# Half of the first layer's columns as seven products of quarters, in the third and later tiles of an attention and feed-forward kernel

## The chip, the cores and the metric

The kernel runs on one core of one Trainium2 chip. The metric is the device time of one execution in microseconds (us). The engines of the core have names in the profile: PE is TensorE, which multiplies matrices (PEld is its loading of weights), DVE is VectorE, ACT is ScalarE, POOL is GpSimd and SP is SyncE; here POOL and SP mostly issue transfers (DMAs). Each engine works through its own queue in order and waits at semaphores for the others. TensorE writes its results to PSUM, a small memory of eight banks; VectorE and ScalarE read them from there and write to SBUF, the working memory.

## The reference

```python
def _attn_ref(q, k, v, g_norm):                  # 8 batches, 8 heads, 576 rows, 64 columns
    kv = np.einsum('bhsd,bhse->bhde', k, v)
    out = np.einsum('bhsd,bhde->bhse', q, kv)
    rms = np.sqrt(np.mean(out * out, axis=-1, keepdims=True) + 1e-06)
    return out / rms * g_norm

def _moe_ref(x, w_in, w_out):                    # x: 4608 x 512, w_in: 512 x 2048, w_out: 2048 x 512
    h = x @ w_in
    g = h * (1.0 / (1.0 + np.exp(-1.702 * h)))
    return g @ w_out
```

The attention is linear: a 64 x 64 matrix `kv` for each head, multiplied by `q`, and each row of 64 scaled by its root mean square. The heads of a row are then laid side by side to a row `x` of 512, and two layers follow: `h = x @ w_in` with 2048 hidden columns, a gate (an approximate GELU), and `g @ w_out`.

## The kernel before

**Tiles.** The rows of `x` are worked on in tiles of 512: tile t (0 to 7) holds the first 512 rows of batch t, and tile 8 (the last) the 64 rows that are left of each of the eight batches, kept in `x_rem`. The text counts tiles from 0. Everything that TensorE multiplies is in f16, sums are f32.

**A tile.** The first layer (`Hidden`, L437) makes the hidden values transposed, with hidden columns on the partitions. A hidden column group ("column" in what follows, 128 of the 2048, so 16 columns) takes four matmuls of 512 moving columns at L446, one for each quarter `ko` of the 512 inputs, added up in one PSUM bank. ScalarE then applies the gate from PSUM into `gT` at L455. The columns run in the order 0, 8, 1, 9, and so on (L590).

The second layer (`Seven`, L463) is already a Strassen scheme for all tiles but the first. The 512 x 2048 by 2048 x 512 product is cut into quarters (256 rows, 1024 hidden values, 256 output columns) and done as seven products instead of eight. A product needs sums and differences of quarters: those of `w_out` are made once in `tw` (`weight_sum`, L457), those of `gT` for each tile in `gS` by VectorE (`sums`, L474). Each product is 16 matmuls of 256 moving columns at L551. The products run in the order 1, 5, 6, 2, 7, 3, 4 and share three PSUM banks: x collects products 1, 6, 7 and 4, y holds product 2, z products 5 and 3. After products 1, 5 and 6 ScalarE copies a bank to SBUF (`keep`, L521) as s1, s5 and s2; after products 2, 7 and 3 VectorE adds the kept part to the bank and writes the output tile `osb` (`place`, L529); after product 4 ScalarE copies the bank (L532). So TensorE must wait before it adds to a bank that is still being read.

**Attention between.** While tile t is worked on, the attention of batch t + 1 is made, in pieces that are hung into the order of the two layers by hand: `units1` after the i-th column of the first layer, `units2` after the n-th matmul of the second (112 in all). In the first layer these are the transposing DMA of q (`transpose_q`, L248), the repacking of k (`pack_k`, L218, two copies of VectorE into `kpad`), four blocks of `kv` (L226, nine small matmuls each; after the last one VectorE casts the result in four pieces, L246), and the loads of k, v and q for batch t + 2 on POOL's queue (L107 and L123). In the second layer these are four `rows` (L288, q times kv, then a square on ScalarE), their sums (L305), the roots (L315), `turn` (L320, scaling by VectorE and a transposing DMA to the next tile's x), and the left-over rows (`out`, `ss`, `apply`), which end in a write to `x_rem` at L360. Tile 7 has nothing left to prepare, and tile 8 neither.

**Scaling by g_norm.** In tiles 0 and 1 `g_norm` is multiplied into x. During the second layer of tile 1 it is multiplied into `w_in` instead, one quarter `ko` at a time (`scale_w_in`, L196): one quarter by ScalarE after matmul 48, three by VectorE after 80, 92 and 100. From tile 2 on x is left unscaled.

**Queues.** The order on every engine is the order of the program text (`manual_schedule`); semaphores come from the tiles' readers and writers. PSUM's eight banks are shared out as three for `ps_a` ("att"), three for `ps_h` ("hT") and two for `ps_o` ("o"). The output of a tile goes out on SP's queue, which also issues the transposing DMAs.

```python
        cols = range(FO) if deep else [f for i in range(HF) for f in (i, HF + i)]
        ready = {} if deep else {8: (0, 4), 13: (4, 6), 15: (6, 8, (0,))}
```

These two lines give the order of the columns and the column after which VectorE forms which part of `gS`.

Of the kernel before, what the change touches and what calls it, by code (L numbers as in the profile page):

```python
# [7 lines left out]
F16 = mybir.dt.float16  # L8
F32 = mybir.dt.float32
# [3 lines left out]
P = 128  # L13
# [3 lines left out]
def kernel(  # L17
# [61 lines left out]
    x_rem = const.tile([P, KO, B * R], F16)  # L79
    HF, HN = FO // 2, DM // 2  # L80
    tw = const.tile([P, 4, HF, HN], F16)


    raw = {"k": kraw, "q": qraw, "v": vbuf}
# [50 lines left out]
    first = {}  # L135
    for n in "kqv":
        if n != "q":
            rows = stage.tile([P, H, J * D], F32, name="qf", tag="qf")
# [298 lines left out]
    class Hidden:  # L437
# [16 lines left out]
        def gate(self, fo):  # L454
            nc.scalar.activation(self.gT[:, fo, :], self.h[fo], AFT.Gelu_apprx_sigmoid)  # L455

    def weight_sum(n):  # L457
        b11, b12 = w_out_sb[:, 0:HF, 0:HN], w_out_sb[:, 0:HF, HN:DM]
        b21, b22 = w_out_sb[:, HF:FO, 0:HN], w_out_sb[:, HF:FO, HN:DM]
        a, b = ((b12, b11), (b22, tw[:, 0]), (b22, b12), (b21, tw[:, 1]))[n]  # L460
        nc.vector.tensor_sub(tw[:, n], a, b)

    class Seven:  # L463
# [5 lines left out]
        def __init__(self, t, gT):  # L469
            self.t, self.gT = t, gT  # L470
            self.s = spool.tile([P, 4, HF, 2 * P], F16, name="gS", tag="gS")
            self.bank, self.kept = {}, {}

        def sums(self, i0, i1, which=(0, 1, 2, 3)):  # L474
            lo, hi = slice(i0, i1), slice(HF + i0, HF + i1)
# [39 lines left out]

        def keep(self, name, mo, as_):
            ps, m = self.ready(name, mo)
            if as_ not in self.kept:
                self.kept[as_] = attn.tile([P, 2, HN], F32, name=as_, tag=as_, bufs=1)
            if ps is not None:  # L520
                nc.scalar.copy(self.kept[as_][:, m], ps)  # L521

# [18 lines left out]

        def run(self, units2):
            n = 0
            for p in self.LAST if self.t == B else self.ORDER:
                name = {1: "x", 6: "x", 7: "x", 4: "x", 2: "y", 5: "z", 3: "z"}[p]
                split = self.t == B and name == "x"
                for mo in range(2):
                    o = self.banks(name, mo)
                    for i in range(HF):
                        a, w = self.operands(p, mo, i)  # L550
                        nc.tensor.matmul(  # L551
                            o,
                            a,
                            w,
                            start=(p in (1, 2, 5) and i == 0 and (mo == 0 or split)),
                            stop=(i == HF - 1),
                            skip_group_check=True,
                        )
                        if i == HF - 1:
                            step, *args = {  # L560
                                1: (self.keep, "s1"),
                                5: (self.keep, "s5"),
                                6: (self.keep, "s2"),
                                2: (self.place, "s1", 0, 0),
                                7: (self.place, "s5", 1, 1),
                                3: (self.place, "s2", 0, 1),
                                4: (self.place, None, 1, 0),
                            }[p]
                            step(name, mo, *args)
                        for u in units2.get(n, ()):  # L570
                            u()
                        n += 1

    def store_rest(mo, n0, n1):
        osb = osbs[B]
        for g in range(2):
# [6 lines left out]
            queue = (nc.sync, nc.scalar)[g]  # L583
            queue.dma_start(out=rows, in_=osb[g * R : (g + 1) * R, mo, n0:n1])

    def dense(t, units1, units2, group, deep, hid=None):
        hid = hid or Hidden(t)
        gT = hid.gT
# [3 lines left out]
        if group and t:  # L592
            order = [(ko, fo) for part in ((0, 3, 1, 2), range(4, group)) for ko in (0, 1) for fo in part]
            order += [(ko, fo) for ko in range(2, KO) for fo in range(group)]
            for ko, i in order:
                pool = (ps_h, "hT") if i < 3 else (ps_a, "att") if i == 3 else (ps_o, "o")
                hid.mm(ko, cols[i], *pool)
            for i in range(group):
                hid.gate(cols[i])
        for i, fo in enumerate(cols):  # L600
# [27 lines left out]
        if deep:  # L628
            steps = [(mo, 4 * i + k) for i in range(3) for mo in range(4) for k in range(4)]
            steps += [(mo, f + k) for f in (12, 14) for mo in range(2) for k in range(2)]  # L630
            steps += [(mo, 12 + k) for mo in (2, 3) for k in range(4)]
            for n, (mo, fo) in enumerate(steps):
                project(mo, fo)
                for u in units2.get(n, ()):
                    u()
        else:
            later = {6: [lambda: seven.sums(6, 8, (1,))], 30: [lambda: seven.sums(6, 8, (2, 3))]}
            for n, us in units2.items():
                later.setdefault(n, []).extend(us)
            seven.run(later)  # L640
# [102 lines left out]
    load_w_out(12, 14)  # L743
    load_w_out(14, FO)

    osbs = {}
    HALVED = (2, 3, 4, 5, 6)
    live = {0: a0}

    def start(b):  # L750
        live[b] = Second(b) if b == 1 else Attention(b)

    for t in range(NT):
# [3 lines left out]
        def at1(i, f, *args):  # L757
            u1.setdefault(i, []).append(lambda: f(*args))

        def at2(i, f, *args):  # L760
            u2.setdefault(i, []).append(lambda: f(*args))  # L761
# [28 lines left out]
        elif b < B:  # L790
            if t == 1:
# [60 lines left out]
```

## Time and profile before

| what | us |
|---|---|
| median of 3 runs (lowest, highest) | 277.36 (276.86, 277.59) |
| the profiled execution's own time | 278.32 |
| its span in the profile | 276.5 |
| TensorE busy | 268.6 (97%) |
| ScalarE busy | 165.9 (60%) |
| VectorE busy | 139.6 (50%) |
| first layer of tile 4, from its first matmul to the second layer's (134.80 to 149.66) | 14.86 |
| second layer of tile 4 (149.66 to 163.24) | 13.58 |
| first and second layer of tile 7, which has no attention work | 13.82 and 12.22 |

The profile is one execution. Its span goes from the first to the last instruction; what lies around it (1.82 us here) belongs to the measured time as well. A row of the groups gives line, engine, operation, output and inputs with their shapes and a count, then the busy time in all and the mean time of one in ns, then the idle time of the engine just before such an operation and what ended it. A row of the timeline or of the chain begins with start and length in us. The granted clock of TensorE was 0.993 of full speed over the span.

### The profile page before, as it was taken

Reading aid. Unit: us, or ns where it says so; the run is one execution under the profiler, and the core shown is the slowest. Engines: PE = TensorE matmul, PEld = TensorE weight load, DVE = VectorE, ACT = ScalarE, POOL = GpSimd, SP = SyncE. Lnnn points to the kernel's source line nnn. Section 1 sums busy time; section 2 is a strip of 40 time slices with the busy share of each in tenths; the row PEclk is TensorE's granted clock in tenths of the full one; section 3 lists DMA queues with packets and bytes.
Section 4 is the critical chain, followed back from the end, with each engine's and each line's share of the span. In section 5 each row is a group of like instructions: output and inputs, shape, how many; then the busy total and the mean of one; then the engine's idle time right before and its main releaser. Section 6 shows DMA issues by size and latency. Waiting matters only on the chain.

```text
span 276.5 us, 5263 instructions
## 1 busy us (share of the span) xinstructions
PE 268.6 (97%) x2160; PEld 173.8 (63%) x2160; DVE 139.6 (50%) x267; ACT 165.9 (60%) x281; POOL 49.9 (18%) x82
## 2 busy tenths in 40 slices
PE   8899999999999999999999999999999999999993
PEld 6434554458755786578646874687458845874682
DVE  1633364948653863377436742675167405222522
ACT  3568609858856765666566656675668466226610
POOL 8762353114010401040104010400000000000000
PEclk9989999999999999999999999999999999999999
DMA  8999999999659876968696869596600510011005
GB/s 173 183 199 204 205 204 199 257 148 156 94 106 216 119 112 153 190 96 114 131 205 108 110 145 208 85 120 180 137 0 2 151 76 2 0 79 76 1 2 152
DMA packets 56539, 35.27 MB, mean 128 GB/s; under 512 B 31810, under 2 KB 53826, under 8 KB 56386
## 3 DMA queue, kind: packets, MB, share of 16 engines
q0 software_dynamic: 25184, 17.91, 46.0%
q1 hardware_dynamic: 30848, 16.49, 24.3%
q10 hardware_dynamic: 482, 0.52, 0.6%
q8 instruction: 17, 0.28, 0.4%
q14 instruction: 8, 0.07, 0.1%
HBM read 36.70 MB, written 9.44 MB: 167 GB/s over the span
## 4 chain that ended last, share of the span: by engine, by line
PE 88%; ACT 3%; DMA 2%; DVE 2%; POOL 2%; issue 1%; DVEq 0%
PE hT L446 45%; PE o L551 32%; PE o L617 4%; PE kvp L230 3%; DMA w_in_sb<-in_moe_w_in_dram 2%; PE outR L294 2%; PE ss L342 1%; DVE x L322 1%; POOL qraw L90 1%; DVE w_in_sb L201 1%; ACT L761 0%; POOL kraw L90 0%; POOL vbuf L90 0%; PE outT L265 0%; DVE osb L529 0%
## 5 line engine op out<-in xcount | busy, mean ns | idle before, releaser
L446 PE MATMUL hT<-xT,w_in_sb 128*128 128x512 f16 x512 | 117.4, 381 | 1.0 <-DMA w_in_sb<-in_moe_w_in_dram 0.9
L455 ACT ACTIVATE gT<-hT 128x512 f16<-128x512 f32 x144 | 84.5, 601 | 40.9 <-PE hT L446 40.9
L446 PEld LDWEIGHTS <-w_in_sb 128*128 128x128 f16 x576 | 54.8, 98 | 62.6 <-issue 1.5
L485 DVE TENSOR_TENSOR gS<-gT 128x512 f16<-128x512 f16 (+1 forms) x48 | 24.4, 509 | 58.1 <-ACT gT L455 57.9
L551 PEld LDWEIGHTS <-gS 128*128 128x128 f16 x512 | 49.7, 98 | 5.8
L551 PE MATMUL o<-tw,gS 128*128 128x256 f16 x384 | 47.4, 273 | 0.0
L551 PEld LDWEIGHTS <-gT 128*128 128x128 f16 x384 | 37.1, 98 | 5.6
L551 PE MATMUL o<-w_out_sb,gT 128*128 128x256 f16 x256 | 33.5, 273 | 0.0
L529 DVE TENSOR_TENSOR osb<-o,s 128x512 f32<-128x512 f32 (+1 forms) x25 | 16.6, 665 | 15.0 <-issue 9.7
L109 POOL DMA_DIRECT2D kraw<-in_k_dram x16 | 9.9, 619 | 67.6 <-DVE kpad L221 61.6
L109 POOL DMA_DIRECT2D vbuf<-in_v_dram x16 | 9.7, 610 | 54.8 <-PE kvp L230 49.4
L521 ACT COPY s<-o 128x512 f32<-128x512 f32 (+1 forms) x26 | 14.3, 550 | 6.5 <-PE o L551 6.4
L344 ACT ACTIVATE ln<-ss,eps_t 128x512 f32<-128x512 f32 (+1 forms) x16 | 9.3, 581 | 14.7 <-PE ss L342 14.6
L322 DVE TENSOR_TENSOR x<-outR,sum 128x512 f16<-128x512 f32 x24 | 14.9, 684 | 6.1 <-ACT sum L318 6.1
L308 DVE TENSOR_REDUCE sum<-sq 128x8 f32<-128x512 f16 x24 | 16.2, 682 | 2.7 <-ACT sq L302 2.5
L246 DVE CAST kvd<-kvp 64x256 f16<-64x256 f32 x24 | 10.1, 422 | 13.9 <-PE kvp L230 13.6
L617 PE MATMUL o<-w_out_sb,gT 128*128 128x512 f16 x64 | 16.7, 379 | 0.0
L302 ACT ACTIVATE sq<-outR 128x512 f16<-128x512 f32 x24 | 14.4, 600 | 3.7 <-PE outR L294 3.7
L761 ACT ACT_TABLE_LOAD x12 | 15.4, 1283 | 0.2
L551 PE MATMUL o<-w_out_sb,gS 128*128 128x256 f16 x128 | 15.4, 272 | 0.0
L551 PE MATMUL o<-tw,gT 128*128 128x256 f16 x128 | 15.3, 273 | 0.0
L280 ACT ACTIVATE sq<-outT 128x512 f16<-128x512 f32 (+1 forms) x16 | 7.8, 493 | 12.3 <-PE outT L260 12.1
(76 smaller groups left out, 217.0 us busy)
## 6 DMA issues: line engine op xcount, KB each, us to landing
out_dram<-osb SPq DMA_DIRECT2D x10, 512.0 KB, 3.0
kraw<-in_k_dram POOLq DMA_DIRECT2D x12, 288.0 KB, 7.0
vbuf<-in_v_dram POOLq DMA_DIRECT2D x12, 288.0 KB, 4.8
qraw<-in_q_dram POOLq DMA_DIRECT2D x3, 512.0 KB, 8.3
qbuf<-in_q_dram POOLq DMA_DIRECT2D x3, 512.0 KB, 8.0
out_dram<-osb SPq DMA_DIRECT2D x6, 192.0 KB, 5.9
w_in_sb<-in_moe_w_in_dram POOLq DMA_DIRECT2D x4, 256.0 KB, 7.8
w_out_sb<-in_moe_w_out_dram POOLq DMA_DIRECT2D x2, 512.0 KB, 14.4
```

The lines of the kernel that those rows point to most:

```text
L109: nc.gpsimd.dma_start(out=raw[n][l * PH : (l + 1) * PH, c0:c1, 0 : NH * D], in_=srcs[n][b].rearrange("(c l) (p j) d -> l p c (j d)", l=2, ...
L302: nc.scalar.activation(sq, t, AFT.Square)
L308: nc.vector.tensor_reduce(out=self.sum4[:, j, :], in_=self.o[j][1].rearrange("p (x d) -> p x d", d=D), op=ALU.add, axis=mybir.AxisListType.X,)
L322: nc.vector.tensor_mul(self.x16[:, j0 : j0 + 2, c0 : c0 + DM // 2].rearrange("p l (h d) -> p h l d", d=D), self.o[j][0].rearrange("p (h l ...
L446: nc.tensor.matmul(self.h[fo], w_in_sb[:, ko, fo * P : (fo + 1) * P], self.x[:, ko], start=(ko == 0), stop=(ko == KO - 1),)
L455: nc.scalar.activation(self.gT[:, fo, :], self.h[fo], AFT.Gelu_apprx_sigmoid)
L485: op(s[:, n, lo], a, b)
L521: nc.scalar.copy(self.kept[as_][:, m], ps)
L529: nc.vector.tensor_add(o, ps, self.kept[with_][:, m])
L551: nc.tensor.matmul(o, a, w, start=(p in (1, 2, 5) and i == 0 and (mo == 0 or split)), stop=(i == HF - 1), skip_group_check=True,)
L617: nc.tensor.matmul(os[mo], gT[:, fo, mo * P : (mo + 1) * P], w_out_sb[:, fo, :], start=(fo == 0), stop=(fo == FO - 1),)
L761: u2.setdefault(i, []).append(lambda: f(*args))
```

## The change

From tile 2 on, eight of the sixteen columns of the first layer are no longer made one by one. Columns 2, 3, 10, 11 form one group and 6, 7, 14, 15 another (`PARTS`). In a group the product of a 512 x 512 piece of `w_in` with the tile's x is cut into quarters (256 inputs, 256 hidden values, 256 rows) and done as seven products of four matmuls with 256 moving columns each, in place of sixteen matmuls with 512 (`SevenIn`). A half column of the other eight (two matmuls of 512) stands between any two products (`hid_seven`).

The products need sums of quarters of `w_in` (`ws`, formed once by VectorE in the second layer of tile 1, `w_in_sum`) and differences of quarters of x (`xS`, formed by VectorE for each tile near the end of the second layer before, `Sums`). After products 1 and 6 ScalarE copies a bank to SBUF, after product 5 VectorE does; after products 2, 7 and 3 VectorE adds the kept part to the bank in SBUF and ScalarE applies the gate from there; after product 4 ScalarE applies it from the bank.

Around it some pieces move. `scale_w_in` on VectorE goes from matmuls 80, 92, 100 to 58, 65, 72. In tiles from 2 on the units of the first layer are counted in the 30 new steps: `transpose_q` and `pack_k` after step 3 instead of column 2, the kv blocks after steps 8, 10, 12 and 14 instead of columns 9 to 12, the loads after step 15 instead of column 13. The parts of `gS` are formed after other steps. The kept sums of both layers lie in the rotating tile "qf" of two buffers, and the second layer asks for its bank z first.

```diff
@@ declarations
+    KH, TH = KO // 2, SM // 2
+    PARTS = (2, 6)
+    ws = const.tile([P, 4, KH, 2 * len(PARTS) * P], F16)
@@ new functions
+    def quarters(w, f, k):
+        hi = slice(HF * P + f.start, HF * P + f.stop)
+        lower = slice(KH + k.start, KH + k.stop)
+        return w[:, k, f], w[:, lower, f], w[:, k, hi], w[:, lower, hi]
+
+    def w_in_sum(n):
+        for g, i in enumerate(PARTS):
+            a11, a12, a21, a22 = quarters(
+                w_in_sb, slice(i * P, (i + 2) * P), slice(0, KH)
+            )
+            o = [ws[:, m, :, 2 * g * P : 2 * (g + 1) * P] for m in range(4)]
+            op, a, b = (
+                (nc.vector.tensor_add, a21, a22),
+                (nc.vector.tensor_sub, o[0], a11),
+                (nc.vector.tensor_sub, a11, a21),
+                (nc.vector.tensor_sub, a12, o[1]),
+            )[n]
+            op(o[n], a, b)
+
+    class Sums:
+        def __init__(self, t):
+            x = xT[t] if t < B else x_rem.rearrange("p c (j r) -> p c j r", j=J)
+            self.x = [[x[:, k : k + KH, n : n + 2, :] for n in (0, 2)] for k in (0, KH)]
+            self.t = spool.tile([P, 4, KH, TH], F16, name="xS", tag="xS")
+
+        def form(self):
+            (b11, b12), (b21, b22) = self.x
+            t = [self.t[:, n].rearrange("p c (j r) -> p c j r", r=P) for n in range(4)]
+            for n, (a, b) in enumerate(((b12, b11), (b22, t[0]), (b22, b12), (b21, t[1]))):
+                nc.vector.tensor_sub(t[n], a, b)
+
+    class SevenIn:
+        ORDER = (1, 5, 6, 2, 7, 3, 4)
...
+        def gate(self, r, n, src):
+            to = slice(self.i + r * HF, self.i + r * HF + 2)
+            nc.scalar.activation(
+                self.gT[:, to, n * TH : (n + 1) * TH], src, AFT.Gelu_apprx_sigmoid
+            )
+
+        def product(self, p):
+            name = {1: "x", 6: "x", 7: "x", 4: "x", 2: "y", 5: "z", 3: "z"}[p]
+            if name not in self.bank:
+                pool, tag = (ps_o, "o") if name == "x" else (ps_a, "att")
+                self.bank[name] = pool.tile([P, 2, TH], F32, name="h7", tag=tag)
+            o = self.bank[name]
+            for a in range(2):
+                for k in range(KH):
+                    w, x = self.operands(p, a, k)
+                    nc.tensor.matmul(o[:, a], w, x, ...)
+            s = self.kept
+            if p == 1:
+                nc.scalar.copy(s["s1"], o)
+            elif p == 5:
+                nc.vector.tensor_copy(s["s5"], o)
+            elif p == 6:
+                nc.scalar.copy(s["s2"], o)
+            elif p == 4:
+                self.gate(1, 0, o)
+            else:
+                which, r, n = {2: ("s1", 0, 0), 7: ("s5", 1, 1), 3: ("s2", 0, 1)}[p]
+                nc.vector.tensor_add(s[which], o, s[which])
+                self.gate(r, n, s[which])
@@ the second layer: kept sums and banks
-            self.bank, self.kept = {}, {}
+            self.bank, self.kept = {}, None
...
-            if as_ not in self.kept:
-                self.kept[as_] = attn.tile([P, 2, HN], F32, name=as_, tag=as_, bufs=1)
+            if self.kept is None:
+                k = stage.tile([P, 6, HN], F32, name="qf", tag="qf")
+                self.kept = {s: k[:, 2 * i : 2 * i + 2] for i, s in enumerate(("s1", "s5", "s2"))}
...
             n = 0
+            self.banks("z", 0)
@@ the first layer of tile 2 and later
+    def hid_seven(t, hid, seven, units1):
+        pairs = [i for i in range(HF) if all(i not in (g, g + 1) for g in PARTS)]
+        halves = [(f, k) for i in pairs for f in (i, HF + i) for k in (0, KH)]
+        xs = xsums.pop(t)
+        steps = [halves[0], halves[1]]
+        for g in range(len(PARTS)):
+            part = SevenIn(hid, xs, g)
+            for n, p in enumerate(part.ORDER):
+                steps += [(part, p), halves[2 + g * len(part.ORDER) + n]]
+        for n, (f, k) in enumerate(steps):
+            if isinstance(f, SevenIn):
+                f.product(k)
+            else:
+                for ko in (k, k + 1):
+                    hid.mm(ko, f)
+                if k:
+                    hid.gate(f)
+            for u in units1.get(n, ()):
+                u()
+            which = {17: 0, 20: 1, 23: 2, 26: 3}.get(n)
+            if which is not None:
+                seven.sums(0, 4, (which,))
+        seven.sums(4, 8, (0,))
...
-            later = {6: [lambda: seven.sums(6, 8, (1,))], 30: [lambda: seven.sums(6, 8, (2, 3))]}
+            i = 4 if t >= SEVEN else 6
+            later = {6: [lambda: seven.sums(i, 8, (1,))], 30: [lambda: seven.sums(i, 8, (2, 3))]}
@@ where the pieces hang
-                at2(80, scale_w_in, 0, nc.vector)
-                at2(92, scale_w_in, 2, nc.vector)
-                at2(100, scale_w_in, 3, nc.vector)
-            f0 = 5 if t == 1 else 2
+                at2(58, scale_w_in, 0, nc.vector)
+                at2(65, scale_w_in, 2, nc.vector)
+                at2(72, scale_w_in, 3, nc.vector)
+                for n, at in ((2, 76), (0, 86), (1, 92), (3, 97)):
+                    at2(at, w_in_sum, n)
+            f0 = 5 if t == 1 else 3
+            late = 14 if t == 1 else 15
...
-                at1(14 if t == 1 else 13, load_kv, t + 2)
-                at1(14 if t == 1 else 13, load_q, t + 2)
+                at1(late, load_kv, t + 2)
+                at1(late, load_q, t + 2)
...
-                at1((10 if t == 1 else 9) + c, of(b, "kv", c))
+                at1(10 + c if t == 1 else 8 + 2 * c, of(b, "kv", c))
...
+            at2(100, form_sums, b)
+        elif t < B:
+            at2(100, form_sums, b)
```

More of the change, by code (lines that the diff above doesn't have):

```diff
@@ L137 @@
         if n != "q":
-            rows = stage.tile([P, H, J * D], F32, name="qf", tag="qf")
+            rows = stage.tile([P, 6, 2 * P], F32, name="qf", tag="qf")
             rows = rows.rearrange("p h x -> p (h x)")[0:PE_]
@@ new lines, with __init__, operands @@
+    class SevenIn:
+        ORDER = (1, 5, 6, 2, 7, 3, 4)
+        def __init__(self, hid, xs, g):
+            self.gT, self.xs, self.g, self.i = hid.gT, xs, g, PARTS[g]
+            self.bank = {}
+            k = stage.tile([P, 6, TH], F32, name="qf", tag="qf")
+            s12 = k[:, 0:4].rearrange("p (a n) c -> p a n c", n=2)
+            self.both = s12
+            self.kept = {"s1": s12[:, :, 0], "s2": s12[:, :, 1], "s5": k[:, 4:6]}
+        def operands(self, p, a, k):
+            f = slice((self.i + a) * P, (self.i + a + 1) * P)
+            g = slice((2 * self.g + a) * P, (2 * self.g + a + 1) * P)
+            a11, a12, a21, a22 = (w[:, 0] for w in quarters(w_in_sb, f, slice(k, k + 1)))
+            (b11, b12), (b21, b22) = [[x[:, k] for x in row] for row in self.xs.x]
+            t = [self.xs.t[:, n, k] for n in range(4)]
+            return {
+                1: (a11, b11),
+                2: (a12, b21),
+                3: (ws[:, 3, k, g], b22),
+                4: (a22, t[3]),
+                5: (ws[:, 0, k, g], t[0]),
+                6: (ws[:, 1, k, g], t[1]),
+                7: (ws[:, 2, k, g], t[2]),
+            }[p]
+        def gate(self, r, n, src):
[12 more added lines that the diff above has]
+                    w, x = self.operands(p, a, k)
+                    nc.tensor.matmul(
+                        o[:, a],
+                        w,
+                        x,
+                        start=(p in (1, 2, 5) and a == 0 and k == 0),
+                        stop=(k == KH - 1),
+                        skip_group_check=True,
+                    )
+            s = self.kept
[11 more added lines that the diff above has]
+                self.gate(r, n, s[which])
@@ L599, in dense @@
                 hid.gate(cols[i])
+        if t >= SEVEN:
+            hid_seven(t, hid, seven, units1)
+            cols = ()
         for i, fo in enumerate(cols):
@@ L744, with form_sums @@
     load_w_out(14, FO)
-    osbs = {}
+    osbs, xsums = {}, {}
+    SEVEN = 2
     HALVED = (2, 3, 4, 5, 6)
     live = {0: a0}
+    def form_sums(t):
+        xsums[t] = Sums(t)
+        xsums[t].form()
     def start(b):
```

## The prediction

> **What bounds the kernel now.** I read the busy shares first, then the chain that ended last, then the groups, then the timeline of one tile.
>
> ```profile
> span 276.5 us, 5263 instructions
> PE 268.6 (97%) x2160; PEld 173.8 (63%) x2160; DVE 139.6 (50%) x267; ACT 165.9 (60%) x281; POOL 49.9 (18%) x82
> PE 88%; ACT 3%; DMA 2%; DVE 2%; POOL 2%; issue 1%; DVEq 0%
> ```
>
> TensorE is busy for 97% of the span and carries 88% of the chain: time goes only if TensorE gets less to do, and comes back wherever TensorE waits.
>
> The chain in order of time (start, length, what) prices its work:
>
> ```profile
> 77.08 0.60 DVE osb L529
> 77.68 0.67 DVE w_in_sb L201
> 78.40 8.16 PE hT L446 x37
> ...
> 134.80 8.63 PE hT L446 x40
> 143.44 0.26 PE kvp L230 x9
> ...
> 220.12 13.81 PE hT L446 x64
> 233.94 12.23 PE o L551 x112
> ```
>
> A first layer without attention work is 64 matmuls in 13.81 us, 215.8 ns each (512 columns). A second layer, already made of 256-column matmuls, is 112 in 12.23, 109.2 ns each. The first rows show the one place where the vector engine already holds TensorE up, the end of the second tile. From the third tile on the steady tiles follow each other every 28.44 us (106.36, 134.80, 163.24).
>
> The groups give durations, the timeline the pace:
>
> ```profile
> L446 PEld LDWEIGHTS <-w_in_sb 128*128 128x128 f16 x576 | 54.8, 98 | 62.6 <-issue 1.5 <-DMA w_in_sb<-in_moe_w_in_dram 1.0 <-DVE w_in_sb L201 0.6
> L529 DVE TENSOR_TENSOR osb<-o,s 128x512 f32<-128x512 f32 x23 | 15.8, 686 | 14.4 <-issue 9.7 <-PE o L551 4.7
> L350 ACT ACTIVATE rs<-ln 128x512 f32<-128x512 f32 x8 | 5.0, 630 | 0.2
> ...
> 143.10 0.69 DVE L485 TENSOR_TENSOR gS<-gS,gT 128x1024 f16<-128x1024 f16 x1
> 143.71 0.68 DVE L485 TENSOR_TENSOR gS<-gT 128x1024 f16<-128x1024 f16 x1
> 147.11 1.74 DVE L246 CAST kvd<-kvp 64x256 f16<-64x256 f32 x4 [2.12 <-PE kvp L230]
> 149.70 0.60 ACT L455 ACTIVATE gT<-hT 128x512 f16<-128x512 f32 x1 [0.27 <-PE hT L446]
> 150.20 0.59 ACT L302 ACTIVATE sq<-outR 128x512 f16<-128x512 f32 x1
> ```
>
> An operation that waits for nothing starts before its predecessor's record ends: 143.10 to 143.71, and 149.70 to 150.20. So the pace of VectorE is some 0.08 us shorter than the duration (0.60 for 0.69), that of ScalarE 0.10 (0.50 for 0.60). What waits for a result pays the whole duration and about 0.03.
>
> **The change, part by part.**
>
> *TensorE, removed and added.* In each of tiles 2 to 8 (counted from 0) two groups of four hidden columns cost 16 matmuls of 512 columns, 16 x 215.8 = 3.45 us. They become seven products of 4 matmuls of 256 columns: 28 x 109.2 = 3.06 us. That is 0.395 us a group, 14 groups, **-5.53 us**. The unknown is the price of a product. Its ends are 107.9 ns (half of 215.8) and 207 ns (109.2 with a 98 ns weight load in the open). The low end would save another 0.5 us in all; the high end is rival B. I take 109.2, because the second layer runs the same shape, one weight load per matmul, through the same waits between products.
>
> The row shows a narrow matmul at half a wide one. The Trainium skill, "TensorE: Matmul & The Clock Gate", section "Back-to-back issue gap", says that in a stream of load and matmul pairs both set the pace, about 81 ns at 128 columns and 131 at 512. By that an estimate for 256 is 98 ns, a group 28 x 98 against 16 x 131, 0.65 us dearer, and the change would cost 9.1 us. The trace's 215.8 and 109.2 contradict it.
>
> *ScalarE, added.* Per group two copies (0.58 as the row of L521, 0.48 of pace): 14 x 2 x 0.48 = 13.4 us in all. The gates stay 16 a tile; six of them now read sums in SBUF. The nearest row with such a source is L350, 630 ns against 601: 0.03 each.
>
> *VectorE, added.* Per group one copy and three adds out of PSUM (0.69, pace 0.60); per tile four differences of x (128x512 f16, 0.42, pace 0.34); eight weight sums of that size once. About 6.2 us a tile. A steady tile has 5.4 busy in the first layer and 10.6 in the second by the windows of the trace, so the engine has room; what counts is order. I walk the queues of a steady tile, time from its first matmul; a product or a half column is 0.43 us, a kv block 0.26.
>
> First group. p1 ends at 1.30, its copy on ScalarE (behind the gate of column 0) at 2.14; p6 writes that bank at 2.60: 0.4 to spare. p6 ends 3.04, copy at 3.9, p7 needs it at 4.63. p7's add ends at 6.0, p4 comes at 6.9. The x differences run on VectorE from 0.9 before to 0.6 after the start, behind the add of the second layer's p3, and are first used at 1.74. The kv blocks, moved from columns 9 to 12 to steps 8, 10, 12 and 14, need kpad, repacked by 2.1, at 3.9. No wait.
>
> Second group. The fourth kv block ends at 7.8, and VectorE then has no pause: four kvd casts 1.74, gate sum 0.60, copy of p5 0.60, gate sum 0.63, add of p2 0.60, gate sum 0.63, and p7's add 0.69. It ends at 13.28. p4 is ready to overwrite that bank at 13.24: **0.1 us of waiting** with the semaphore. This place decides: every delay on VectorE lands here one for one.
>
> Second layer. p7's gate starts at 13.31, four gates follow at 0.50, the last column's gate ends at 15.9. Then VectorE's sum of columns 4 to 7 takes 0.69, to 16.6; p5 of the second layer needs it at 14.2 + 1.75 (p1) + 0.44 (two rows of attention) + 0.44 = 16.8. It just fits. In tiles 7 and 8 there are no rows of attention, p5 comes at 16.4 and waits **0.4 us**, load included.
>
> Five tiles (2 to 6) at about 0.1, the first 0.2: +0.6. Tiles 7 and 8: +0.8. The slower gates push the chain by 0.03 each: +0.2. If differences of a strided x lost their pace and cost as much as a PSUM add, tile 2 and its kpad would pay another 1 us; the gate sums with a similar stride cost 0.42, and I take that.
>
> *End of tile 1.* Scaling w_in moves ahead of p7's add (two operations, 1.3 us), two weight sums with it (0.7). That add ends 0.4 late for p4: +0.4. After it six weight sums, an add, four x differences and two kpad copies stand in a row; kpad ends 0.3 late for the first kv of tile 2: +0.3. The wait of 0.61 for L201 in tile 2 goes, because scaling is over long before: together **+0.1**.
>
> *Costed at nothing.* The rotating buffer that both layers' kept products now share: each reuse lies a whole group or layer behind its last reader. The x pool and out stores: SP's order is unchanged. Loads of k, v and q for the tile after next: on POOL's queue v and q follow the last kv block and start near 7.8 instead of 12.7; k waits for kpad and starts 1 to 2 us later than now. They now share the DMA engines with the qTd transpose, which starts at 1.3 and lands 8.8 to 10.5 us later, by 11.8; its reader comes at 14.4. That cover is 2.6 us; were the transpose to lose more, the rest would show at the rows of attention.
>
> *Sum.* -5.53 + 0.6 + 0.8 + 0.2 + 0.1 = -3.8 us. The profiled execution took 278.32 (span 276.5, 1.8 around it), 0.96 over the median of 277.36. I apply the difference to the median: **273.5 us**.
>
> **The rivals.**
>
> *A. VectorE's chain paces at full durations.* The mechanism: the operations between the last kv block and p7's add each wait for a semaphore, so none overlaps its predecessor. The casts already show it (1.74 for four of 0.42), the sums L485 do not. Eight operations at 0.11 make p4 0.9 late, five tiles 4.5 us; the gates behind it delay p5 in tiles 7 and 8 by some 0.5 each. That is 5.5 on 273.5: **279.0**, slower than before. It decides from 0.77 us of delay a steady tile (3.8/5).
>
> *B. Products cost more than 109.2.* Each product starts behind a wait, and if its first weight load stood in the open, 98 products x 0.098 = 9.6 us, **283.1**. Against it: in tile 7 the second layer's 112 matmuls with their waits leave no gap. Break-even is 9.7 ns on each of 392 matmuls. The Trainium skill's section named above would land on this side.
>
> *C. All of it shows.* If the copies and adds are a little quicker than their rows, no new wait stays: **271.8**. The margin at p4 is one tenth, so this is possible.
>
> *D. The gain is eaten.* Half of A's delay, some 0.5 to 0.9 a tile: within 0.3%, 276.5 to 278.2. As nothing but the first layer changes shape, "the change does nothing" has no other form here.
>
> **How the numbers follow.** Forecast (272.6 to 275.2) 55%; C 12%; between forecast and D (275.2 to 276.5) 13%; D 7%; A 10%; B 3%. 0.3% of 277.36 is 0.83 us, about what a measurement of this kernel can tell from no change. Faster 0.80, same 0.07, slower 0.13. The range 271.7 to 276.7 holds the forecast, most of C, the case between and a sliver of D: 8 in 10.
>
> **What would show it.** The product line has 392 matmuls at a pace of 109 ns; steady tiles are 27.7 to 27.8 us apart instead of 28.44; TensorE waits for VectorE's p7 add at p4 of the second group by 0.1 to 0.2, and for the gate sums by 0.4 in the last two tiles only; the wait for L201's line is gone. Wrong would be steady tiles over 28.2 with the wait at p4 near 0.7 (A), a product pace over 115 (B), or waits at the qTd rows.

## The result, and the profile after

The changed kernel takes 281.68 us (median of 4 runs, 281.27 to 282.46) against 277.27 for the kernel before beside it: a ratio of 1.0163, 95% interval [1.0134, 1.0192]. The forecast was 273.5 with a range up to 276.7; it was wrong in sign. The profiled execution took 281.31, its span is 279.5. Medians in this document are of all runs of a kernel; ratios are to the kernel before run beside it, with slow runs (over 1.5% above the fastest of their kernel) left out, so they are not exactly the ratios of the medians.

The head of the profile page of the changed kernel, its shares of the chain, and its row of TensorE's granted clock in 40 slices:

```profile
span 279.5 us, 5714 instructions
PE 264.6 (95%) x2328; PEld 190.5 (68%) x2328; DVE 185.2 (66%) x331; ACT 173.2 (62%) x309; POOL 50.1 (18%) x82
PEclk9999999999999979999999999999999999999999
PE 78%; DMA 8%; DVE 5%; ACT 4%; POOL 2%; issue 1%; DVEq 0%; ACTq 0%
```

TensorE is busy for 264.6 us, 4.0 less than the 268.6 of before, so the work did get less. But its part of the chain fell from 88% to 78%, and 8% is now a DMA. One slice, the fifteenth of 40 (97.8 to 104.8), has the clock at 0.7. Both belong to one place, which the chain in order of time shows (start, length, what):

```profile
77.51 0.86 PE hT L449 x4
79.24 0.44 PE h L538 x4
82.02 15.32 DMA qTd<-qbuf
97.39 0.60 PE outR L297 x4
...
112.56 0.86 PE hT L449 x4
...
140.39 0.86 PE hT L449 x4
```

By the chain, tile 2 runs from 77.51 to 112.56, 35.05 us; the next takes 27.83. In tile 2 the first rows of attention (L297) wait for the transposing DMA of q, issued at 82.02. The waits of TensorE name it, with their sum, number and longest:

```profile
PE outR L297 <- DMA qTd<-qbuf: 5.2, 1, 5.2
```

The preceding two matmuls of L656 start at 91.82 and the rows at 97.39, so 5.35 us are lost beyond their 0.22. What follows is slow as well. Stretches of the trace give start and end, length, busy time and count of PE, PEld, DVE, ACT and POOL, then the granted clock, the DMA share and GB/s:

```profile
97.40:100.80 3.40, 3.40 (x21) 2.65 (x22) 1.72 (x3) 1.19 (x2) 0.00 (x0) 0.50 1.33 155
100.80:104.20 3.40, 3.40 (x37) 3.09 (x36) 2.21 (x5) 2.86 (x4) 0.00 (x0) 1.00 0.00 0
```

For 3.41 us after the idle stretch TensorE has half its clock, which costs half of that, 1.7 us. The Trainium skill, "TensorE: Matmul & The Clock Gate", section "What's actually happening", in its table of two states, says that the clock falls to half after at least one idle window of about 3.4 us; that agrees with this row.

5.35 + 1.7 = 7.05, and 281.31 - 7.05 = 274.3, where the forecast's sum stood at 274.5 for a profiled execution (278.32 - 3.8). So one wait in one tile is nearly the whole miss, 7.05 of the 8.2 us between the forecast and the median. That 274.3 and 274.5 agree so closely is in part luck: the profiled execution of the kernel before ran its start at half clock for 3.42 us (13.11 to 16.53, granted clock 0.50), which the changed one did not. The times of the tiles do not depend on that. The time of each tile, from its first matmul to the next tile's (of tile 8 to its last matmul), in us; the last two columns are experiments told below:

| tile | before | changed | q first | q first, sums later |
|---|---|---|---|---|
| 1 | 29.43 | 29.91 | 29.90 | 29.91 |
| 2 | 28.74 | 35.05 | 28.05 | 27.87 |
| 3 to 6, each | 28.44 | 27.83 | 27.83 | 27.65 |
| 7 | 26.04 | 25.63 | 25.64 | 25.48 |
| 8 | 25.93 | 25.53 | 25.53 | 25.38 |

**What is different around the transpose.** First the timeline of SP's queue in the changed kernel, then POOL's, both from tile 2; after them the same two transfers of POOL before the change:

```profile
77.84 4.07 SPq L781 DMA_DIRECT2D out_dram<-osb  x8
82.02 6.35 SPq L253 DMA_TRANSPOSE qTd<-qbuf  x1
...
80.90 1.40 POOL L112 DMA_DIRECT2D kraw<-in_k_dram  x2 [16.29 <-DVE kpad L224]
85.58 1.22 POOL L112 DMA_DIRECT2D vbuf<-in_v_dram  x2 [3.28 <-PE kvp L233]
```
```profile
81.92 5.52 SPq L250 DMA_TRANSPOSE qTd<-qbuf  x1
...
79.29 1.40 POOL L109 DMA_DIRECT2D kraw<-in_k_dram  x2 [14.06 <-DVE kpad L221]
90.49 1.22 POOL L109 DMA_DIRECT2D vbuf<-in_v_dram  x2 [9.80 <-PE kvp L230]
```

In tile 2, unlike the later ones, eight stores stand ahead of the transpose on SP's queue (two in tile 3), so it is issued 4.5 us after the tile's start (82.02 against 77.51); in tile 3 it is 1.2 (113.72 against 112.56). That is so in both kernels. What the change moves in tile 2 is on the other queue: the k loads start at 80.90 instead of 79.29, because kpad now stands behind the weight sums and x differences on VectorE, and the v loads at 85.58 instead of 90.49.

The transpose moves packets of 256 bytes, the loads packets of 512 and more. The packets in the stretch 86 to 90 before the change, and 90 to 97 after it:

```profile
DMA packets 2524, 0.78 MB, mean 196 GB/s; under 512 B 2416, under 2 KB 2448, under 8 KB 2524
```
```profile
DMA packets 1156, 0.77 MB, mean 110 GB/s; under 512 B 544, under 2 KB 1155, under 8 KB 1155
```

Before the change the 2304 packets of qTd and qTr all pass in these four microseconds, most of them in the quiet between the landing of k (87.61) and the issue of v. In the changed kernel k lands at 89.20 and v, issued at 85.58, follows directly; by the packet records 1714 of the 2304 pass by 90, and the last 590 need over seven microseconds more. The v loads suffer too: from issue to landing they take 11.2 us in the median, where they took 5.1 before.

Tile 3 of the changed kernel waits for no transpose. Its rows, SP's queue and POOL's:

```profile
113.72 3.23 SPq L253 DMA_TRANSPOSE qTd<-qraw  x1
120.42 1.22 POOL L112 DMA_DIRECT2D vbuf<-in_v_dram  x2 [4.11 <-PE kvp L233]
```

There v is issued 6.70 us behind the transpose, not 3.56, and k (114.90) behind it too, not ahead of it.

### The profile page after: what moved, and what is told of

Its sections match the earlier page's. It is cut to its first block, busy times and chain, and to the rows that moved or that the text cites. A ratio compares the mean times of both kernels' runs of the same rounds, so it can differ in the third digit from the quotient of the medians.

```text
span 279.5 us, 5714 instructions
## 1 busy us (share of the span) xinstructions
PE 264.6 (95%) x2328; PEld 190.5 (68%) x2328; DVE 185.2 (66%) x331; ACT 173.2 (62%) x309; POOL 50.1 (18%) x82
## 4 chain that ended last, share of the span: by engine, by line
PE 78%; DMA 8%; DVE 5%; ACT 4%; POOL 2%; issue 1%; DVEq 0%; ACTq 0%
PE o L656 30%; PE hT L449 24%; PE h L538 13%; DMA qTd<-qbuf 5%; PE o L750 4%; DMA w_in_sb<-in_moe_w_in_dram 3%; PE kvp L233 2%; PE outR L297 2%; DVE gS L588 2%; ACT gT L525 1%; POOL qraw L93 1%; PE ss L345 1%; ACT gT L458 1%; DVE w_in_sb L204 1%; DVE x L325 1%
## 5 line engine op out<-in xcount | busy, mean ns | idle before, releaser
L449 PE MATMUL hT<-xT,w_in_sb 128*128 128x512 f16 x320 | 85.4, 379 | 1.0 <-DMA w_in_sb<-in_moe_w_in_dram 1.0
L458 ACT ACTIVATE gT<-hT 128x512 f16<-128x512 f32 x88 | 50.8, 600 | 12.1 <-PE hT L449 12.1
L656 PEld LDWEIGHTS <-gS 128*128 128x128 f16 x512 | 49.6, 98 | 6.7 <-DVE gS L588 0.9
L656 PE MATMUL o<-tw,gS 128*128 128x256 f16 x384 | 47.8, 273 | 0.3 <-DVE gS L588 0.3
L449 PEld LDWEIGHTS <-w_in_sb 128*128 128x128 f16 x352 | 32.6, 98 | 18.8 <-DMA w_in_sb<-in_moe_w_in_dram 1.4
L656 PEld LDWEIGHTS <-gT 128*128 128x128 f16 x384 | 37.8, 100 | 6.5 <-issue 0.4
L525 ACT ACTIVATE gT<-qf 128x512 f16<-128x512 f32 x42 | 26.4, 628 | 18.6 <-DVE qf L557 18.3
L557 DVE TENSOR_TENSOR qf<-h,qf 128x512 f32<-128x512 f32 x42 | 28.3, 687 | 10.7 <-PE h L538 10.4
L656 PE MATMUL o<-w_out_sb,gT 128*128 128x256 f16 x256 | 34.8, 280 | 0.0
L538 PEld LDWEIGHTS <-ws 128*128 128x128 f16 x224 | 21.9, 98 | 14.5
L588 DVE TENSOR_TENSOR gS<-gT 128x1024 f16<-128x1024 f16 (+1 forms) x34 | 22.3, 655 | 13.8 <-ACT gT L458 13.6
L538 PE MATMUL h<-xS,ws 128*128 128x256 f16 x168 | 25.2, 273 | 0.0
L538 PEld LDWEIGHTS <-w_in_sb 128*128 128x128 f16 x168 | 16.4, 98 | 11.9 <-issue 1.9
L633 DVE TENSOR_TENSOR osb<-o,qf 128x512 f32<-128x512 f32 (+1 forms) x25 | 16.6, 664 | 11.7 <-issue 6.4
L625 ACT COPY qf<-o 128x512 f32<-128x512 f32 (+1 forms) x26 | 14.5, 558 | 5.4 <-PE o L656 5.4
L656 PE MATMUL o<-tw,gT 128*128 128x256 f16 x128 | 15.3, 273 | 0.3 <-DVE osb L633 0.3
```

The source lines that it names most:

```text
L449: nc.tensor.matmul(self.h[fo], w_in_sb[:, ko, fo * P : (fo + 1) * P], self.x[:, ko], start=(ko == 0), stop=(ko == KO - 1),)
L525: nc.scalar.activation(self.gT[:, to, n * TH : (n + 1) * TH], src, AFT.Gelu_apprx_sigmoid)
L538: nc.tensor.matmul(o[:, a], w, x, start=(p in (1, 2, 5) and a == 0 and k == 0), stop=(k == KH - 1), skip_group_check=True,)
L557: nc.vector.tensor_add(s[which], o, s[which])
L588: op(s[:, n, lo], a, b)
L633: nc.vector.tensor_add(o, ps, self.kept[with_][:, m])
```

## The experiments

The theory to be tested, "both sides": the transpose needs a stretch without loads; the change closes it in front (k later) and behind (v and q earlier). Rivals: the early v and q loads alone, k's lateness alone, or the products themselves. The v and q loads are moved together in every run, so which of the two matters is not separated.

**The v and q loads late again.** The changed kernel; in tile 2 the kv blocks come at steps 16 to 22 and the loads after step 23.

```diff
-            late = 14 if t == 1 else 15
+            late = 14 if t == 1 else 23 if t == 2 else 15
-                at1(10 + c if t == 1 else 8 + 2 * c, of(b, "kv", c))
+                at1(10 + c if t == 1 else (16 if t == 2 else 8) + 2 * c, of(b, "kv", c))
```

> The changed kernel with the four kv blocks of tile 2 alone after steps 16, 18, 20 and 22 instead of 8, 10, 12 and 14, and its loads after step 23; so the v and q loads start about 3 us later, when the qTd transpose of tile 2 has nearly finished. Theory C (collision: the early v and q loads run into the late transpose, TensorE waits 5.35 us for it, and its clock is halved for 3.41 us after): both go, 281.7 - 5.35 - 1.7 = about 274.6. Rival S (the transpose is slow for a reason before it: eight stores, the k loads, which also start 1.6 us later than in the kernel before): the wait stays, about 281.7. Rival P (the seven products or VectorE's extra work slow the transpose): 281.7 as well.

Measured: 275.42, ratio 0.9938 [0.991, 0.9966]. v is issued at 90.98 and TensorE no longer waits for qTd. VectorE's four casts now stand directly ahead of p7's add, and p4 of the second group waits 1.65 in this tile, as the prediction's "every delay on VectorE lands here" says.

**The transpose ahead of the stores.** The changed kernel; the q transposes of batch 3 are issued at matmul 104 of tile 1's second layer.

```diff
-            at1(f0, start, b)
-            at1(f0, of(b, "transpose_q"))
+            if t != 2:
+                at1(f0, start, b)
+                at1(f0, of(b, "transpose_q"))
+            if t == 1:
+                at2(104, start, 3)
+                at2(104, of(3, "transpose_q"))
```

> The changed kernel with the two transposing DMAs of q for batch 3 (used in tile 2) issued near the end of the second layer of tile 1, ahead of the eight output stores on the queue; nothing else moves, the early loads stay. Theory C: the transpose is over before the v loads begin at 85.6, no wait in tile 2, about 274.6; the stores end some 5 us later, which nobody reads. Rival P (products and VectorE's work slow it to 15 us): it begins some 5.5 us sooner and takes 15, so it would land close to its reader at 92 and a rest of the wait of up to 1 us may stay: 274.6 to 276. If transposing is slow as such beside k loads, the same.

Measured: 274.26, ratio 0.9871 [0.9843, 0.9899]. qTd is issued at 73.18, qTr lands at 78.97, no rows wait for it, and no loads were moved:

```profile
73.18 1.68 SPq L253 DMA_TRANSPOSE qTd<-qbuf  x1
75.04 1.86 SPq L255 DMA_TRANSPOSE qTr<-qrem  x1
78.12 4.03 SPq L781 DMA_DIRECT2D out_dram<-osb  x8
```

This beats both kernels, and it is 3.4 us under the 277.64 of the kernel before in that comparison.

**Early v and q loads alone.** The kernel before; in tile 2 the kv blocks come at columns 4 to 7 and the loads after column 8.

```diff
-                at1(14 if t == 1 else 13, load_kv, t + 2)
-                at1(14 if t == 1 else 13, load_q, t + 2)
+                late = 14 if t == 1 else 8 if t == 2 else 13
+                at1(late, load_kv, t + 2)
+                at1(late, load_q, t + 2)
-                at1((10 if t == 1 else 9) + c, of(b, "kv", c))
+                at1((10 if t == 1 else 4 if t == 2 else 9) + c, of(b, "kv", c))
```

> The kernel before, with one part of the change alone: in tile 2 the kv blocks come after columns 4 to 7 instead of 9 to 12 and the loads after column 8, so that the v and q loads start near 85.5 instead of 90.5. No seven products in the first layer. Theory C: the transpose of q, issued at 82, is caught by the loads as in the changed kernel and lands near 97 with its reader at 93: 4 us of wait and 1.7 us of halved clock, 277.3 + 5.7 = about 283. Rivals S and P: nothing of this, 277.3.

Measured: 277.76, ratio 0.9985 [0.9953, 1.0017]: nothing. So the early loads alone are not the cause, and the simple form of the theory fell. Here k was issued at 78.08 and landed at 86.07, and the 2048 packets of qTd passed between 85 and 88, just ahead of v's data. This led to "both sides".

**TensorE kept busy through the wait.** The changed kernel with 22 matmuls of 512 columns put ahead of tile 2's first rows, into the bank that the rows then overwrite.

```diff
+            if self.b == 3 and i == 0:
+                for _ in range(22):
+                    nc.tensor.matmul(t, w_out_sb[:, 0, 0:P], w_out_sb[:, 0, :], start=True, stop=True)
```

> The changed kernel with 22 matmuls of 512 columns (4.75 us of TensorE) put in front of the first rows of attention in tile 2, into the bank that these rows overwrite; they fall into the wait of 5.35 us. If the halved clock after the wait costs what the records say (3.41 us at half speed, 1.7 us) and comes from the idle time: 281.7 - 1.7 = about 280.0, with the wait then 0.6 and no halved clock. If the slow matmuls after the wait have another cause (the transfers that are still running): 281.7.

Measured: 278.88, 2.8 under the changed kernel. The half clock is gone; the 22 matmuls take 4.75 and the rows then start at once, so the data was there at least 0.6 sooner than in the changed kernel's profile. Tile 2 takes 32.79 instead of 35.05, which is 1.7 + 0.6; the other 0.5 of the 2.8 lies outside this tile and is unassigned. That the slow stretch comes from the idle time and not from the products is shown: it goes when the idle time is filled with work that nothing needs.

**k early, v and q early.** The changed kernel; the repacking of k that frees the buffer for the next k loads is done at matmul 31 of tile 1's second layer.

```diff
-            at1(f0, start, b)
+            if t != 2:
+                at1(f0, start, b)
+            if t == 1:
+                at2(31, start, 3)
+                at2(31, of(3, "pack_k"))
...
-            at1(f0, of(b, "pack_k"))
+            if t != 2:
+                at1(f0, of(b, "pack_k"))
```

> The changed kernel with the repacking of k for batch 3 moved from step 3 of tile 2 to matmul 31 of tile 1's second layer, so that the k loads of batch 4 start near 69 instead of 80.90 and are out of the way when the q transpose starts; the v and q loads stay early (85.6). Theory 'both sides' (the transposes lose their quiet stretch to the end of the k loads in front and to the v and q loads behind): they have from about 86.4 to 87.5 or later alone, the wait at rows(0) falls from 5.35 to under 2 us, the half clock goes, 274.5 to 276.5. Rival 'v and q alone' (with the transpose issued behind the stores, early v and q loads are enough): the wait stays above 4 us, 280 to 282. Rival 'k alone': no wait, 274.6.

Measured: 274.41, ratio 0.9909 [0.9883, 0.9934]. v is issued at 85.49, as early as in the changed kernel, and the wait is gone altogether:

```profile
81.90 3.00 SPq L253 DMA_TRANSPOSE qTd<-qbuf  x1
85.07 1.17 SPq L255 DMA_TRANSPOSE qTr<-qrem  x1
68.16 1.40 POOL L112 DMA_DIRECT2D kraw<-in_k_dram  x2 [4.15 <-DVE kpad L224]
85.49 1.22 POOL L112 DMA_DIRECT2D vbuf<-in_v_dram  x2 [15.94 <-PE kvp L233]
```

Without k packets the first packet of the transpose moves 1.2 us behind its issue, where it took 4.8 in the changed kernel, and the last one by 87. Taking away the front side alone is enough, as taking away the back side was.

**Both moves without the products.** The kernel before with the early v and q loads as above, and `pack_k` done twice in tile 2, 1.53 us more on VectorE, so that k is issued later too.

```diff
...
             at1(f0, of(b, "pack_k"))
+            if t == 2:
+                at1(f0, of(b, "pack_k"))
...
```

> The kernel before with both halves of the change's move in tile 2 and none of its products: kv blocks at columns 4 to 7 and loads after column 8 as in the run before with early v and q loads (277.76, no effect), and the repacking of k done twice, 1.53 us more on VectorE, so that the k loads start 1.5 later, as in the changed kernel. Theory 'both sides': the wait at the first rows appears, 2 to 5 us, with the half clock behind it if it is longer than 3.4: 280 to 284. If the products or the gates are needed for the wait, the time stays near 277.8 and rows(0) waits for nothing.

Measured: 278.91, ratio 1.0049 [1.0029, 1.0069]. The wait appears, in a kernel that has none of the change's arithmetic. The waits of this kernel:

```profile
PE outR L294 <- DMA qTd<-qbuf: 1.0, 1, 1.0
```

It is 1.16 by the starts of the matmuls, below the 2 to 5 expected, as the time is below the 280 to 284, and no half clock follows.

**k late alone.** The kernel before with only `pack_k` done twice.

```diff
             at1(f0, of(b, "pack_k"))
+            if t == 2:
+                at1(f0, of(b, "pack_k"))
```

> The kernel before with only the repacking of k in tile 2 done twice, so that the k loads start 1.5 us later (near 80.8 instead of 79.29) and v and q stay late (90.5). Theory 'both sides': the stretch between the end of k (near 89) and the arrival of v (near 92) stays quiet, the transposes run there and land near 91.5, rows(0) at 92.8 waits for nothing or at most 0.3: 277.4 to 278.0. Rival 'k alone': a wait of several us, 280 or more.

Measured: 277.76, ratio 1.0006 [0.9985, 1.0026]: nothing. k lands 8.15 us behind the issue of qTd, later than in the changed kernel (7.18), but v is issued only at 89.38 and qTr lands at 90.84. So neither side alone does it; the two together do.

**Both moves, v a little sooner.** What was open is the size, 1.16 against 5.35. In the run with both moves v is issued 4.32 behind qTd, in the changed kernel 3.56. Here the kv blocks and loads come one column earlier than in that run, against which the edit is shown.

```diff
-                late = 14 if t == 1 else 8 if t == 2 else 13
+                late = 14 if t == 1 else 7 if t == 2 else 13
-                at1((10 if t == 1 else 4 if t == 2 else 9) + c, of(b, "kv", c))
+                at1((10 if t == 1 else 3 if t == 2 else 9) + c, of(b, "kv", c))
```

> As the run with both loads moved in the kernel before (k 1.5 later, v and q early: a wait of 1.16 and 278.91), and the kv blocks and the loads behind them one column earlier still, columns 3 to 6 and after column 7. There v was issued 4.32 behind qTd (85.44 against 81.12); in the changed kernel it is 3.56 (85.58 against 82.02). This makes it 3.5 to 3.7, and kv waits up to 0.4 for kpad. Theory 'the lead decides' (what the transpose has not moved when the v loads arrive trickles among them): the wait at the first rows grows from 1.16 to 3 to 5.5 us, with half clock behind it if it exceeds 3.4: 280.5 to 285. If the products' share in the wait is something else, it stays near 1.2 and the time near 279.

Measured: 285.83, ratio 1.0304 [1.0267, 1.0342]. The rows in the timeline of TensorE, and the stretch behind them:

```profile
97.72 0.61 PE L294 MATMUL outR<-kvd,qTd 128*128 128x128 f16 x4 [5.24 <-DMA qTd<-qbuf]
```
```profile
97.30:100.60 3.30, 2.88 (x18) 2.33 (x19) 1.02 (x2) 1.12 (x2) 0.00 (x0) 0.50 1.67 125
```

The wait is 5.41 and the half clock lasts 3.41 us: the changed kernel's loss, reproduced without a single product. Tile 2 takes 35.75 instead of 28.74, and the time is above the 280.5 to 285 expected. 0.66 us of lead (4.32 to 3.66) made 4.25 us of wait.

**v a little later in the changed kernel.** The same step the other way: kv blocks and loads of tile 2 two steps later.

```diff
-            late = 14 if t == 1 else 15
+            late = 14 if t == 1 else 17 if t == 2 else 15
-                at1(10 + c if t == 1 else 8 + 2 * c, of(b, "kv", c))
+                at1(10 + c if t == 1 else (10 if t == 2 else 8) + 2 * c, of(b, "kv", c))
```

> The changed kernel with tile 2's kv blocks after steps 10, 12, 14 and 16 instead of 8, 10, 12 and 14, and the loads after step 17, so that v is issued 0.86 later, 4.4 behind qTd instead of 3.56, and k as before. Theory 'the lead decides': the wait at rows(0) falls from 5.35 to between 0.5 and 2.5 and the half clock goes; VectorE's casts stand 0.86 closer to p7's add, which may cost p4 up to 0.9 in this tile: 275 to 278. If 0.86 of lead does not matter, 281 to 282 with the wait above 4.

Measured: 278.28, ratio 0.9983 [0.9947, 1.002]; its ten executions lie between 275.2 and 282.4, and the one profiled is the longest of them. The median is just above the 275 to 278 expected. In the profile p4 waits 1.05 for the casts, and the rows as long as before:

```profile
97.82 0.61 PE L297 MATMUL outR<-kvd,qTd 128*128 128x128 f16 x4 [5.08 <-DMA qTd<-qbuf]
```

So the wait expected between 0.5 and 2.5 was 5.25 in this execution. By the median the 0.65 us of lead is worth 3.4 us. The spread of 7.2 us, against 1.8 in the 13 executions of the kernel before beside it, suggests that this point is an edge, where some executions win and some lose. That is not shown: the wait in the short ones was not profiled.

**The order of VectorE behind the kv casts.** The kernel with the transpose ahead of the stores, and two of the gate sums later, so that the third stands behind p7's add. The edit is shown against that kernel.

```diff
-            which = {17: 0, 20: 1, 23: 2, 26: 3}.get(n)
+            which = {17: 0, 20: 1, 25: 2, 27: 3}.get(n)
```

> The changed kernel with tile 2's q transposes issued ahead of the stores (274.26 by the run before), and in the first layer of tiles 2 to 8 the gate sum 2 after step 25 instead of 23, behind VectorE's p7 add, and sum 3 after step 27. If the waits of TensorE at p4 of the second group (0.18 to 0.19 in five tiles) come, as the prediction walked them, from VectorE's queue (kvd casts, copy of p5, sums, p7's add), the add starts 0.63 earlier and they go: 5 x 0.19 = 0.95. The two waits at p5 of the second layer in tiles 7 and 8 (0.32 each) may stay or grow by up to 0.3, as the later sums follow one another more closely. Expected 273.3, between 272.7 and 273.9. If p4 waits for something else (ScalarE's gate, the weight load), the time stays at 274.3 and the waits of 0.19 stay.

Measured: 273.1, ratio 0.9858 [0.9838, 0.9877], the fastest of all. The end of the first layer of a steady tile, timeline of TensorE, in the changed kernel and then in this one:

```profile
153.00 0.59 PE L449 MATMUL hT<-xT,w_in_sb 128*128 128x512 f16 x2
153.62 0.60 PE L538 MATMUL h<-xS,w_in_sb 128*128 128x256 f16 x4
```
```profile
145.48 0.59 PE L449 MATMUL hT<-xT,w_in_sb 128*128 128x512 f16 x2
145.91 0.60 PE L538 MATMUL h<-xS,w_in_sb 128*128 128x256 f16 x4
```

From the half column to p4 it is 0.62 in the one and 0.43, two matmuls of 215.8, in the other: the 0.19 of waiting is gone in all five tiles. The waits at p5 in tiles 7 and 8 fell from 0.32 to 0.21. 5 x 0.19 + 2 x 0.11 = 1.17, and 274.26 - 273.1 = 1.16.

All runs beside each other: times of issue, landing and wait in us from each profile. "lead" is v's issue less qTd's. Tile 2 begins between 76.2 and 79.4 in these profiles, so times of different rows are compared as differences within a row.

| kernel | qTd issued | k landed | lead | qTr landed | wait at the rows |
|---|---|---|---|---|---|
| before | 81.92 | 87.61 | 8.57 | 89.89 | 0 |
| changed | 82.02 | 89.20 | 3.56 | 98.42 | 5.35 |
| v, q late again | 84.07 | 91.58 | 6.91 | 96.84 | 0 |
| q first | 73.18 | 88.16 | 12.68 | 78.97 | 0 |
| k early | 81.90 | 74.01 | 3.59 | 89.95 | 0 |
| before, v, q early | 80.71 | 86.07 | 4.26 | 91.53 | 0 |
| before, k late | 80.75 | 88.90 | 8.63 | 90.84 | 0 |
| before, both | 81.12 | 89.06 | 4.32 | 94.72 | 1.16 |
| before, both, v sooner | 81.13 | 88.98 | 3.66 | 100.25 | 5.41 |
| changed, v two steps later | 81.91 | 89.33 | 4.21 | 98.94 | 5.25 |

## Why the prediction was wrong

**The product price** was right. With the waits at p4 gone a steady tile takes 27.65 against 28.44: 0.79, two groups at the predicted 0.395. 392 matmuls stand at L538, four in 0.43 to 0.45. Rival B is out.

**p4 of the second group** was predicted at 0.1 in tiles 3 to 6 and measured 0.19, with the cause as walked: moving one sum behind the add removes it. Rival A's 0.9 did not come. **p5 of the second layer** in tiles 7 and 8 was 0.32 for 0.4. **The slower gates** read 628 ns from SBUF (42 of them at L525) against 600 from PSUM, the 0.03 that was taken.

**End of tile 1** was predicted at +0.1 and cost about 0.4. p4 was 0.43 for 0.4, the first kv of tile 2 0.21 for 0.3, and the wait for scaled w_in is gone, but it was not worth 0.61. That figure is idle time of the weight loads; tile 2 of the kernel before took only 0.30 more than a steady one (28.74 against 28.44).

**Costed at nothing** is the step that failed, in its last part. It named the resource (the DMA engines that qTd shares with the loads), the two moves (v and q near 7.8, k later) and the place where a loss would show, the rows of attention. Two figures in it were wrong. "Starts at 1.3" is a steady tile. In tile 2 the row of the kernel before shows the transpose issued at 81.92, 4.5 us after the tile's first matmul at 77.46, behind eight stores. With v at about 8 the overlap was not at the transpose's end but over its body. And "8.8 to 10.5 us later, by 11.8" was the duration beside the k loads alone, with v issued only after the landing; the changed kernel's took over 15 in tile 2. The cover of 2.6 us was thus of another tile, and the price of sharing was taken as small without a row for it. A wait of 5.35 then brought a second term that the working had nowhere: 1.7 for the half clock.

Of the 3.8 us that the sum promised, 3.4 came as soon as the transpose had its place. By the tiles of "q first" it is 3.46: 0.69, four times 0.61 and twice 0.40 gained, 0.47 lost in tile 1. Most of what is missing is the end of tile 1.

## What to carry to other kernels

A cover that is computed from a steady tile holds for the steady tiles; the first tile after a prologue or a change of phase has its own queue in front of each transfer, and its row must be read by itself. When loads are moved, look up what else is in flight at their new time, and price the slowest sharer by what happens if it finishes last, not by its share of the bandwidth. A transfer that is ready early can be issued ahead of stores that nobody waits for: here that one move made the change worth 3.4 us instead of a loss of 4.4.

## What the runs showed of the hardware

*A transposing DMA next to loads does not slow down in proportion.* By the packet records, 256-byte packets took 87 to 156 ns in mean from 90 to 93 us of the changed kernel, where 1000 a microsecond pass at 18 ns each when the loads are away. 544 small packets in seven microseconds stand against 2416 in four. A share of the bandwidth taken by the loads does not explain it: from 91 to 92 all 16 DMA engines together moved 27 packets, 17 GB/s, although some 440 packets of the transposes and most of v were still to come. What the transfers waited for, no run here tells. The Trainium skill, "DMA: Bandwidth & Descriptors", section "Issuing engines are not separate DMA queues", says that transfers from all issuing engines run on the same 16 DMA engines and interleave; the trace has packets of both queues in the same microseconds, loads from POOL (637 packets from 90 to 97) and transposes from SP (518), and does not list the engine of each.

*Loads in flight delay the start of a transpose.* Its first packet moved 4.3 to 4.8 us behind its issue in the kernel before and the changed one, with the k loads in flight, and 1.2 behind it with k out of the way and the same eight stores ahead.

*The loss has an edge.* 0.66 us of lead turned a wait of 1.16 into 5.41, and at a lead of 4.21 executions of one program differed by 7.2 us.

*Idle time costs twice past a point.* Waits of 5.2 to 5.4 came with half clock: for 3.41 us in the changed kernel and with v sooner, for 6.83 us with v two steps later, of which the first 2.1 fell into the wait itself. The wait of 1.16 had none, nor had the 1.65 at p4 with v and q late again.
